# Gated mix of sliding-window attention and SwiGLU FFN: two tail tiles made behind the last exponential, output buffers swapped, WD rows and gate sums moved

## The chip, the core and the metric

One core of a Trainium2 chip runs the kernel. Its engines work side by side, each through its own list of instructions in order: TensorE (PE; PEld is its weight load), VectorE (DVE), ScalarE (ACT), GpSimd (POOL) and SyncE (SP), which here only issues DMAs. The metric is the device time of one launch in microseconds. The median of 3 runs before is 842.95 us (842.54 to 843.75).

## What is computed

```python
# x: 2048 x 512; 32 heads of 16; window 256; FFN width 1792
g = sigmoid((x * gate_w).sum(-1, keepdims=True))
q, k, v = heads(x @ wqkv)
p = softmax(where(0 <= i - j < 256, q @ k.T / 4, -1e9))
a = concat(p @ v) @ wo
b = (silu(x @ w_gate) * (x @ w_up)) @ w_down
out = g * a + (1 - g) * b
```

All is in float32. Every large product is made of three products of a high and a low part (hi·hi, hi·lo, lo·hi), so each operand is first "split": a cast to its high part on ACT (L65) or DVE (L67), and a subtraction for the low part (L68) on DVE or POOL.

## The kernel before

The program is written out in the order in which each engine gets its work; no scheduler reorders it. The sequence 2048 is cut into 4 chunks of 512 columns (CH) or 16 blocks of 128 (NB), the heads into 8 groups of 4 (G), the FFN into 14 tiles of 128 (NF).

**Start** (up to L491). x, the value weights and the first query and key weights are loaded and split; `split_x(c)` splits a chunk's four pieces on ACT and DVE. `vproj(b)` makes the values of a block in a PSUM tile "pb" that ACT copies out (`put_v`, L395). `proj` makes queries and keys of a group; `stack` places them by twelve DMAs (L247, L248) into the slots QT and KT. `first`, the score products of group 0 (L263), is interleaved with the remaining value products.

**Slots** (loop at L595). Slot t = 0 to 127 does the first pass over the scores of group g+1 (L263, row maxima on DVE, L265) and the second pass of group g (L304, exponential on ACT L306, masks on POOL L308 and L311). In the last sixteen slots, t from g7 = 112, there is no first pass left. Four slots share one "unit": a projection of a later group or one side, gate or up, of an FFN tile (L215), 48 pairs of matmuls. A unit's four results are copied to buffers "ev" (ring of 5, `kept()`, L511) and, for the FFN, stored to DRAM (`raws`, L514). `prepare`, at quarter 3 of a unit's first slot, splits the next unit's weights (wh on ACT L65, wl on POOL L68) and fetches the following ones into "raw", a single buffer (L73, raw<-wgu).

At the first slot of each four, `av` multiplies weights and values of a finished chunk (L328) and `finish` post-processes it in five pieces spread over the four slots: ACT copies one PSUM half into "on" (L339), DVE adds the other half (L341), transposes into "ot" (L346), divides (L350, L351), transposes into "on" again (L355), and POOL stores that (od<-on, L356). The pool `osb` had one buffer of each name, so L339 of the next chunk writes the buffer that od<-on reads.

`later(t, hd, f)` places further work behind quarter hd of slot t. In the last slots this is: the gate sums (`gate_fetch` L541, `gate_block` L544, one a slot from slot 111), six rows of WD (`wd_early`: fetch into an "ev" buffer by L73, split on DVE one slot later, L67 and L68), and the first made tile of the tail (`first_tile`, L562: SiLU as exp, +1, reciprocal, two products on POOL, split).

**Tail** (from L633). For c in 4 chunks and n in 14 tiles: `hidden` computes silu(gate)·up from reloaded tiles (`load_kept`, got<-raws, L692) or, for the tile MADE = 2 of the order, from 24 matmuls in PSUM (L703); `halved` splits it (hh on ACT, hl on DVE); `step` multiplies it with WD into four PSUM accumulators (12 matmuls, L83 to L85). Rows of WD that were not loaded early are fetched during chunk 0 and split on DVE and POOL (`load_wd` with raw2), and so are the four pieces of WO on ACT and POOL. Tile 0 of chunk 0 came ready from the slots.

Of the kernel before, what the change touches and what calls it, by code (L numbers as in the profile page):

```python
# [9 lines left out]
F32 = mybir.dt.float32  # L10
F32R = mybir.dt.float32r
AF = mybir.ActivationFunctionType
ALU = mybir.AluOpType
# [20 lines left out]
def gated_mix(ctx, tc, xT, xn, w01, wqk, wv, wo, wgu, wd, gw, out):  # L34
# [54 lines left out]
    def run(gen, n=None):  # L89

        while n is None or n > 0:
            if next(gen, run) is run:
                break
            n = n and n - 1
# [74 lines left out]
    with ExitStack() as A:  # L169
# [163 lines left out]
        def finish(g, c):  # L333


            first, second = AV[g, c]
            both = osb.tile([P, CH], F32, name="on")
            lo = 0 if c else 64
            nc.scalar.copy(both[:, lo:], second[:, lo:])  # L339
            yield  # L340
            nc.vector.tensor_tensor(out=both[:, lo:], in0=first[:, lo:], in1=both[:, lo:], op=ALU.add)  # L341
            if lo:
                nc.vector.tensor_copy(both[:, :lo], first[:, :lo])
            yield
            ot = osb.tile([P, CH], F32, name="ot")
            nc.vector.transpose(ot, both)  # L346
            yield
            v = ot.rearrange("p (s e) -> p s e", e=32)
            rc = osb.tile([P, CH // 32], F32, name="rc")
            nc.vector.reciprocal(rc, v[:, :, DH])  # L350
            nc.vector.tensor_tensor(out=v[:, :, :DH], in0=v[:, :, :DH],  # L351
                                    in1=rc[:, :, None].to_broadcast([P, CH // 32, DH]), op=ALU.mult)
            yield
            on = osb.tile([P, CH], F32, name="on")
            nc.vector.transpose(on, ot)  # L355
            nc.gpsimd.dma_start(od[g, :, c * CH:(c + 1) * CH], on)  # L356
            yield
# [56 lines left out]

        def split_x(c):
            for k in range(NK):
                split(xhi[c][:, k], xlo[c][:, k], xraw[c][k], nc.scalar, nc.vector)
# [27 lines left out]
        prefetch()  # L445
        split_x(1)
        fill_v(vs[1])
        fill_rows(QT[0], 0.0, 1, nc.gpsimd)
        fill_rows(KT[0], -1.0, 1, nc.gpsimd)
        for b in range(2):  # L450
            run(vproj(b))
        split_x(2)
        run(vproj(2))
        run(proj(0, 1, pp, "pa", los=nc.vector))
        stack(0, 0)
# [20 lines left out]
        for n, turn in enumerate(turns):  # L476
            for m, _ in enumerate(turn, 3 * NK * n):
                run(first, 2 * (2 * NB * (m + 1) // total - 2 * NB * m // total))
            if n == 3:
                prepare()  # L480
            if n == 8:
                put_max(0, 0)
            if n == 9:
                get_max(0, 0)
# [7 lines left out]
        ptp = A.enter_context(tc.tile_pool(name="ptp", bufs=13))  # L492
        osb = A.enter_context(tc.tile_pool(name="osb", bufs=1))

# [54 lines left out]

        pieces = [h for t in (*QT[0], KT[0][0], *QT[1], KT[1][0], KT[0][1]) for h in halves_of(t)]  # L550
        GATE0 = g7 - 1
        later(GATE0 - 1, 1, gate_place)
        for b in range(NB):
            later(GATE0 + b - 1, 3, lambda b=b: gate_fetch(b))
            later(GATE0 + b, 3, lambda b=b: gate_block(b))
        for m in range(6):
            wd_early(g7 + 3 + 2 * m, ORDER[m], pieces[m])

        hh0, hl0, g0, u0 = (KT[0][1][:, i * CH:(i + 1) * CH] for i in range(4))
        g0, u0 = g0.bitcast(F32), u0.bitcast(F32)  # L560

        def first_tile():  # L562
            e = kept()
            nc.scalar.activation(e, g0, AF.Exp, scale=-1.0)
            yield
            nc.vector.tensor_scalar(e, e, 1.0, None, op0=ALU.add)
            yield
            nc.vector.reciprocal(e, e)
            yield
            nc.gpsimd.tensor_tensor(out=e, in0=g0, in1=e, op=ALU.mult)  # L570
            yield
            nc.gpsimd.tensor_tensor(out=e, in0=e, in1=u0, op=ALU.mult)
            yield
            split(hh0, hl0, e, nc.scalar, nc.vector)
            yield
        FT = first_tile()

        def first_load():
            nc.sync.dma_start(g0, raws[0, 0, 0])
            nc.sync.dma_start(u0, raws[0, 1, 0])  # L580
        later(g7, 2, first_load)
        for m in (4, 5, 6, 8, 9, 11):
            later(g7 + m // 4, m % 4, lambda: run(FT, 1))

        def gate_done():
# [3 lines left out]
            nc.vector.tensor_scalar(igate, gate, -1.0, 1.0, op0=ALU.mult, op1=ALU.add)  # L589
        later(GATE0 + NB, 3, gate_done)  # L590

# [3 lines left out]
        for t in range(G * NB + 1):  # L595
# [29 lines left out]
            if t >= 10 and t % 4 == 2 and t + 6 < G * NB:  # L625
                load_v((t + 6) // 4)
        prepare()
        run(FIN)
# [4 lines left out]
    with ExitStack() as B:  # L633
# [108 lines left out]

        seq = [(c, n) for c in range(NCH) for n in range(NF)][1:]
        loads = [(c, ORDER[n]) for c, n in seq if n != MADE]
        for _ in range(3):
            load_kept(*loads.pop(0))
        fresh, waiting, ready = [], [(0, 0, hh0, hl0)], []
        for c, n in seq:
            f = ORDER[n]
            todo, ready = ready, []  # L750
            if c == 0 and n + 5 < NF:
                ready.append(load_wd(ORDER[n + 5], pieces[n + 5], raw2(), (nc.vector, nc.gpsimd)))
# [56 lines left out]
```

## Time and profile before

| what | us |
|---|---|
| median of 3 runs | 842.95 |
| the profiled execution | 845.21 |
| its span, first to last instruction | 843.5 |
| start, up to the first slots | about 0 to 90 |
| slots 112 to 127 with their last products | 541.6 to 613.0 |
| tail | 613.0 to 843.5 |
| mean granted clock of TensorE | 0.991 |

How the views are read. A busy line gives time, share of the span and number of instructions. A row of waits reads "engine, tile, line <- what ended the wait: us in total, times, longest". A row of the timeline reads "start, duration, engine, line, operation, tiles, count [idle time before it <- what ended it]". A row of windows reads "stretch, its length, then busy time and count of PE, PEld, DVE, ACT and POOL, granted clock, DMA share, GB/s".

### The profile page before, as it was taken

To read this page: it belongs to the slowest core of one execution; us is meant where nothing else is said; L and a number is where in the kernel's file an instruction comes from. 1 tells how busy PE (TensorE), PEld (TensorE's weight loads), DVE (VectorE), ACT (ScalarE), POOL (GpSimd) and SP (SyncE) were. 2 spreads that over 40 slices of the span, in tenths; PEclk is the share of its full clock that TensorE was granted. 3 is DMA by queue.
4 is the path that set the end of the run, shared out by engine and by line. 5 is a ranking of instruction groups with operands and counts; after the bars stand their busy time and mean duration, and the time that the engine had idled before them with its cause. 6 is when DMAs were issued, how large, how long until landed. Compare 5 with 4: busy or idle time off the path is not lost.

```text
span 843.5 us, 21585 instructions
## 1 busy us (share of the span) xinstructions
PE 826.2 (98%) x8306; PEld 688.2 (82%) x8306; DVE 516.7 (61%) x1416; ACT 448.2 (53%) x935; POOL 362.0 (43%) x645
## 2 busy tenths in 40 slices
PE   8999999999999999999999999999988999999998
PEld 5799988888898888888888888867766888888886
DVE  5496677677577667667667676654558344353433
ACT  6313666666666666656666665645444533344341
POOL 5812546555555646546555554565435211011020
PEclk9999999999999999999999999989999999999999
DMA  8664524534624624533633642546478735473721
GB/s 286 172 199 132 165 104 150 173 112 130 198 91 138 192 106 124 179 137 109 187 131 94 196 149 100 181 140 217 156 277 267 209 131 161 165 212 86 242 72 50
DMA packets 70582, 133.27 MB, mean 158 GB/s; under 512 B 14288, under 2 KB 19024, under 8 KB 70480
## 3 DMA queue, kind: packets, MB, share of 16 engines
q1 hardware_dynamic: 66512, 118.00, 44.9%
q0 software_dynamic: 3968, 13.90, 4.5%
q8 instruction: 65, 1.06, 0.5%
q14 instruction: 37, 0.30, 0.1%
HBM read 61.08 MB, written 45.61 MB: 126 GB/s over the span
## 4 chain that ended last, share of the span: by engine, by line
PE 84%; DMA 5%; POOL 4%; issue 2%; DVE 2%; SPq 2%; ACT 1%; POOLq 0%; ACTq 0%
PE pb L215 22%; PE pa L215 21%; PE pb L328 6%; PE ps L263 6%; PE ps L85 5%; PE ps L83 5%; PE ps L84 5%; PE ps L304 4%; PE pb L85 2%; PE pb L84 2%; PE pb L83 2%; PE ps L328 2%; DMA ev<-wd 1%; PE pb L703 1%; PE pa L703 1%
## 5 line engine op out<-in xcount | busy, mean ns | idle before, releaser
L265 DVE CUSTOM_DVE_ANT_0 ps<-ps,mask 128x384 f32<-128x384 f32 (+2 forms) x512 | 271.8, 539 | 144.3 <-PE ps L263 71.5
L306 ACT ACTIVATE pt<-ps 128x384 f32<-128x384 f32 (+2 forms) x512 | 240.7, 477 | 114.9 <-PE ps L263 56.9
L308 POOL TENSOR_SCALAR_AFFINE_SELECT pt<-pt 128x256 f32<-128x256 f32 x256 | 107.5, 420 | 228.3 <-ACT pt L306 219.8
L304 PE MATMUL ps<-q,k 64*128 64x384 f32 (+2 forms) x512 | 164.4, 330 | 2.4 <-ACT on L339 1.6
L263 PE MATMUL ps<-k,q 63*128 63x384 f32 (+2 forms) x512 | 159.9, 330 | 1.2 <-DMA k<-xhi 1.2
L215 PE MATMUL pb<-xhi,wh 64*128 64x512 f32 x512 | 117.8, 397 | 0.6 <-DVE on L341 0.6
L215 PE MATMUL pb<-xlo,wh 64*128 64x512 f32 x512 | 116.1, 394 | 0.0
L215 PE MATMUL pb<-xhi,wl 64*128 64x512 f32 x512 | 115.7, 394 | 0.0
L215 PE MATMUL pa<-xhi,wh 64*128 64x512 f32 x512 | 114.2, 395 | 0.8 <-ACT ev L511 0.8
L215 PE MATMUL pa<-xlo,wh 64*128 64x512 f32 x512 | 112.7, 393 | 0.0
L215 PE MATMUL pa<-xhi,wl 64*128 64x512 f32 x512 | 112.5, 393 | 0.0
L263 PEld LDWEIGHTS ps<-k,q 63*128 63x128 f32 x512 | 90.1, 185 | 16.0 <-issue 6.9
L304 PEld LDWEIGHTS ps<-q,k 64*128 64x128 f32 x512 | 93.6, 185 | 10.0 <-ACT on L339 2.5
L311 POOL TENSOR_SCALAR_AFFINE_SELECT pt<-pt 128x256 f32<-128x256 f32 x224 | 96.4, 430 | 0.0
L707 DVE TENSOR_TENSOR sg<-got,sg 128x512 f32<-128x512 f32 x51 | 51.3, 1005 | 52.6 <-ACT sg L706 48.2
L328 PE MATMUL ps<-pt,vg 64*32 64x320 f32 (+4 forms) x1408 | 76.5, 351 | 0.0
L328 PE MATMUL pb<-pt,vg 64*32 64x320 f32 (+3 forms) x1360 | 75.6, 356 | 0.0
L265 DVE DVE_READ_ACCUMULATOR2_ANT mx<- 128x1 f32 x512 | 71.5, 140 | 0.0
L328 PEld LDWEIGHTS pb<-pt,vg 64*32 64x32 f32 x1360 | 46.9, 107 | 29.3 <-ACT pt L306 9.9
L215 PEld LDWEIGHTS pb<-xhi,wh 64*128 64x128 f32 x512 | 60.4, 187 | 9.8 <-DVE on L341 1.1
L215 PEld LDWEIGHTS pb<-xhi,wl 64*128 64x128 f32 x512 | 60.5, 186 | 7.4
L215 PEld LDWEIGHTS pa<-xhi,wh 64*128 64x128 f32 x512 | 58.0, 186 | 8.2 <-ACT ev L511 1.9
(163 smaller groups left out, 1592.0 us busy)
## 6 DMA issues: line engine op xcount, KB each, us to landing
raws<-ev SPq DMA_DIRECT2D x104, 256.0 KB
got<-raws SPq DMA_DIRECT2D x102, 256.0 KB
od<-on POOLq DMA_DIRECT2D x32, 256.0 KB, 2.9
raw<-wgu SPq DMA_DIRECT2D x28, 256.0 KB
q<-xhi SPq DMA_DIRECT2D x56, 128.0 KB
k<-xhi SPq DMA_DIRECT2D x56, 128.0 KB
vd<-vs POOLq DMA_DIRECT2D x8, 672.0 KB, 5.0
vg<-vd SPq DMA_DIRECT2D x32, 168.0 KB
```

Source lines behind the costliest of these rows:

```text
L83: nc.tensor.matmul(ps, lh, rh, start=start and i == 0, stop=False)
L84: nc.tensor.matmul(ps, lh, rl, start=False, stop=False)
L85: nc.tensor.matmul(ps, ll, rh, start=False, stop=stop and i == n - 1)
L215: mm = nc.tensor.matmul(ps[me], w[r], x[r], start=not second and i == 0, stop=bool(second) and i == n - 1)
L263: nc.tensor.matmul(ps[:, :n], QT[g % 2][pr][r, q0:q0 + P], KT[g % 2][pr][r, k0:k0 + n], start=True, stop=True)
L265: mx = nc.vector.tensor_tensor_reduce(out=ps[:, :n], in0=ps[:, :n], in1=mask[:, 3 * P - n:], scale=1.0, scalar=NEG, op0=ALU.add, op1=ALU.m ...
L304: nc.tensor.matmul(ps[:, :n], KT[g % 2][pr][r, k0:k0 + P], QT[g % 2][pr][r, k0:k0 + n], start=True, stop=True)
L306: BEHIND.append(nc.scalar.activation(pt[:, j, :n], ps[:, :n], AF.Exp, scale=SCALE))
L308: nc.gpsimd.affine_select(out=pt[:, :, :P], in_=pt[:, :, :P], pattern=[[0, 2], [1, P]], compare_op=ALU.is_ge, fill=0.0, base=0, channel_mu ...
L311: nc.gpsimd.affine_select(out=pt[:, :, 2 * P:], in_=pt[:, :, 2 * P:], pattern=[[0, 2], [-1, P]], compare_op=ALU.is_ge, fill=0.0, base=-1, ...
L328: nc.tensor.matmul(AV[g, c][h][32 * j:32 * j + 32, q0 - c * CH:q1 - c * CH], VG[4 * g + kb // 4][o, kb % 4, 17 * j:17 * j + 32], PT[g, kb, ...
L707: nc.vector.tensor_tensor(out=sg, in0=gu[1], in1=sg, op=ALU.mult)
```

## The change

**Start.** `split_x` takes a range of pieces; chunks 1 and 2 are split two pieces at a time between `vproj(0)`, `vproj(1)` and `vproj(2)`, and `first` begins eight yields of the value products later. ACT, between its copies of the value results (vs_115 and vs_116 are the two value buffers, xhi_74 and xhi_76 the high parts of chunks 1 and 2), as a piece of the difference:

```order
 L65 CAST wh<-vs_116 128x512 x2
-L65 CAST xhi_74<-q_123 128x512 x4
-L395 COPY vs_115<-pb 128x8x4x16 x2
-L65 CAST xhi_76<-k_124 128x512 x4
+L65 CAST xhi_74<-q_123 128x512 x2
+L395 COPY vs_115<-pb 128x8x4x16
+L65 CAST xhi_74<-q_123 128x512 x2
+L395 COPY vs_115<-pb 128x8x4x16
+L65 CAST xhi_76<-k_124 128x512 x2
 L395 COPY vs_116<-pb 128x8x4x16
+L65 CAST xhi_76<-k_124 128x512 x2
 L238 COPY ev<-pa 128x512
```

The first copy has moved ahead of two casts; the third now has two casts behind it, ahead of L238, the copy that feeds `stack`.

**Slots.** In `finish`, all three tiles have the name "on" in a pool of two buffers; "rc" keeps one. Each chunk takes three buffers in turn, so the second half copy of a chunk and its stored result share a buffer, the tile between them has the other, and the next chunk begins with that other one. Nine WD rows instead of six are fetched, at slots 113 to 115, 117 to 119 and 121 to 123, and the order of the places they go to (`pieces`) is changed. The gate sums begin at slot 110. DVE in slots 117 to 121, before (q_87 is a place for WD rows, L544 a gate sum):

```order
L351 TENSOR_TENSOR ot<-ot,rc 128x16x16
L67 CAST q_86<-ev 128x512
L68 TENSOR_TENSOR q_86<-ev,q_86 128x512
L544 SCALAR_TENSOR_TENSOR xhi,gate<-xlo,xhi 128x512
L355 STREAM_TRANSPOSE on<-ot 128x512
L544 SCALAR_TENSOR_TENSOR xhi,gate<-xlo,xhi 128x512
L67 CAST q_87<-ev 128x512
L68 TENSOR_TENSOR q_87<-ev,q_87 128x512
L341 TENSOR_TENSOR on<-pb,on 128x512
L544 SCALAR_TENSOR_TENSOR xhi,gate<-xlo,xhi 128x512
```

and in the same place after (L546 is the gate sum):

```order
L351 TENSOR_TENSOR on<-on,rc 128x16x16
L67 CAST q_87<-ev 128x512
L68 TENSOR_TENSOR q_87<-ev,q_87 128x512
L546 SCALAR_TENSOR_TENSOR xhi,gate<-xlo,xhi 128x512
L355 STREAM_TRANSPOSE on<-on 128x512
L67 CAST k_88<-ev 128x512
L68 TENSOR_TENSOR k_88<-ev,k_88 128x512
L546 SCALAR_TENSOR_TENSOR xhi,gate<-xlo,xhi 128x512
L67 CAST k_88<-ev 128x512
L68 TENSOR_TENSOR k_88<-ev,k_88 128x512
L341 TENSOR_TENSOR on<-pb,on 128x512
L546 SCALAR_TENSOR_TENSOR xhi,gate<-xlo,xhi 128x512
```

One split still stands ahead of L355; behind it there are now two, and the second of them is directly ahead of L341 of the next chunk.

**End of the slots.** `first_tile` is gone. Tiles 0 and 1 of chunk 0 are loaded at slot 126 into the gate's places (XG), their SiLU stands behind the last exponential, at quarter 0 of slot 128, after `prepare` for the last FFN tile (which stood behind the loop), and their product and split at quarter 2. ACT there before, from the last exponential on:

```order
L306 ACTIVATE pt<-ps_10580 128x128
L511 COPY ev<-pa 128x512
L586 ACTIVATE gate<-gate 128x16
L511 COPY ev<-pb 128x512
L339 COPY on<-ps_10607 128x512
L511 COPY ev<-pb 128x512
L65 CAST wh<-raw 128x512
L706 ACT_TABLE_LOAD
L706 ACTIVATE sg<-got_10695 128x512
L65 CAST hh<-sg 128x512
```

and after, behind the last exponential:

```order
L513 COPY ev<-pa 128x512
L585 ACTIVATE gate<-gate 128x16
L65 CAST wh<-raw 128x512
L574 ACT_TABLE_LOAD
L574 ACTIVATE ev<-xhi 128x512
L574 ACTIVATE ev<-xlo 128x512
L513 COPY ev<-pb 128x512
L339 COPY on<-ps_10621 128x512
L65 CAST k_89<-ev 128x512 x2
L513 COPY ev<-pb 128x512
L704 ACTIVATE sg<-pa 128x512
L704 ACTIVATE sg<-got_10711 128x512
```

The table load and two SiLUs (ev<-xhi, ev<-xlo) come ahead of the copies of the last unit's second half (L513, formerly L511) and of L339; the two casts (k_89) come ahead of the last of these copies. The tail starts with tile 2, the 24 products, and steps 0 and 1 follow them on PE; tile 1 is no longer reloaded there, and WD rows 6, 7 and 8 are no longer split there.

The diff, without its renumbering:

```diff
-            ot = osb.tile([P, CH], F32, name="ot")
+            ot = osb.tile([P, CH], F32, name="on")
...
-            rc = osb.tile([P, CH // 32], F32, name="rc")
+            rc = osb.tile([P, CH // 32], F32, name="rc", bufs=1)
...
-        split_x(1)
+        split_x(1, range(2))
         fill_v(vs[1])
         fill_rows(QT[0], 0.0, 1, nc.gpsimd)
         fill_rows(KT[0], -1.0, 1, nc.gpsimd)
-        for b in range(2):
-            run(vproj(b))
-        split_x(2)
+        run(vproj(0))
+        split_x(1, range(2, NK))
+        run(vproj(1))
+        split_x(2, range(2))
         run(vproj(2))
+        split_x(2, range(2, NK))
...
-                run(first, 2 * (2 * NB * (m + 1) // total - 2 * NB * m // total))
+                run(first, 2 * (2 * NB * max(m + 1 - 8, 0) // (total - 8) - 2 * NB * max(m - 8, 0) // (total - 8)))
...
-        osb = A.enter_context(tc.tile_pool(name="osb", bufs=1))
+        osb = A.enter_context(tc.tile_pool(name="osb", bufs=2))
...
-        pieces = [h for t in (*QT[0], KT[0][0], *QT[1], KT[1][0], KT[0][1]) for h in halves_of(t)]
-        GATE0 = g7 - 1
+        pieces = [h for t in (*QT[0], KT[0][0]) for h in halves_of(t)]
+        pieces += [halves_of(t)[hf] for hf in range(2) for t in (*QT[1], KT[1][0])] + halves_of(KT[0][1])
+        GATE0 = g7 - 2
...
-        for m in range(6):
-            wd_early(g7 + 3 + 2 * m, ORDER[m], pieces[m])
+        for m, t in enumerate((1, 2, 3, 5, 6, 7, 9, 10, 11)):
+            wd_early(g7 + t, ORDER[m], pieces[m])
...
-        for m in (4, 5, 6, 8, 9, 11):
-            later(g7 + m // 4, m % 4, lambda: run(FT, 1))
...
+        first_halves = [[KT[0][1][:, (2 * n + i) * CH:(2 * n + i + 1) * CH] for i in range(2)] for n in range(2)]
+        first_sg = []
         def first_load():
+            for n in range(2):
+                for i in range(2):
+                    nc.sync.dma_start(XG[2 * n + i], raws[n, i, 0])
+        def first_silu():
+            for n in range(2):
+                sg = kept()
+                first_sg.append(sg)
+                nc.scalar.activation(sg, XG[2 * n], AF.Silu)
+        def first_tiles():
+            for n, sg in enumerate(first_sg):
+                nc.vector.tensor_tensor(out=sg, in0=XG[2 * n + 1], in1=sg, op=ALU.mult)
+                split(*first_halves[n], sg, nc.scalar, nc.vector)
+        later(g7 + NB - 2, 2, first_load)
+        later(g7 + NB, 0, prepare, first_silu)
+        later(g7 + NB, 2, first_tiles)
...
-        later(GATE0 + NB, 3, gate_done)
+        later(g7 + NB - 1, 3, gate_done)
...
-        prepare()
         run(FIN)
...
-        seq = [(c, n) for c in range(NCH) for n in range(NF)][1:]
+        seq = [(c, n) for c in range(NCH) for n in range(NF)][2:]
...
-        fresh, waiting, ready = [], [(0, 0, hh0, hl0)], []
+        fresh, waiting, ready = [], [(0, n, *first_halves[n]) for n in range(2)], []
...
-            if c == 0 and n + 5 < NF:
+            if c == 0 and 9 <= n + 5 < NF:
```

More of the change, by code (lines that the diff above doesn't have):

```diff
@@ L413, in gated_mix, with split_x @@
         xraw = [[xraw[2 * c + k // 2][k % 2] for k in range(NK)] for c in range(NCH)]
-        def split_x(c):
-            for k in range(NK):
+        def split_x(c, ks=range(NK)):
+            for k in ks:
                 split(xhi[c][:, k], xlo[c][:, k], xraw[c][k], nc.scalar, nc.vector)
@@ L555, in gated_mix @@
             later(GATE0 + b, 3, lambda b=b: gate_block(b))
-        for m in range(6):
-            wd_early(g7 + 3 + 2 * m, ORDER[m], pieces[m])
[L559 to L576, printed above, removed]
-        def first_load():
-            nc.sync.dma_start(g0, raws[0, 0, 0])
-            nc.sync.dma_start(u0, raws[0, 1, 0])
-        later(g7, 2, first_load)
-        for m in (4, 5, 6, 8, 9, 11):
-            later(g7 + m // 4, m % 4, lambda: run(FT, 1))
+        for m, t in enumerate((1, 2, 3, 5, 6, 7, 9, 10, 11)):
+            wd_early(g7 + t, ORDER[m], pieces[m])
+        first_halves = [[KT[0][1][:, (2 * n + i) * CH:(2 * n + i + 1) * CH] for i in range(2)] for n in range(2)]
+        first_sg = []
+        def first_load():
+            for n in range(2):
[13 more added lines that the diff above has]
+        later(g7 + NB, 2, first_tiles)
         def gate_done():
```

## The prediction

> **What bounds the kernel now.** I read the page's busy times first, then who TensorE waits for, then windows around those waits.
>
> ```profile
> span 843.5 us, 21585 instructions
> PE 826.2 (98%) x8306; PEld 688.2 (82%) x8306; DVE 516.7 (61%) x1416; ACT 448.2 (53%) x935; POOL 362.0 (43%) x645
> ```
>
> TensorE (PE) is busy nearly throughout, so an edit pays only where PE stands still or runs slow. PE's own waits:
>
> ```profile
> PE ps L85 <- DVE hl L68: 2.7, 3, 1.5
> PE ps L83 <- ACT hh L65: 2.5, 2, 1.4
> PE ps L304 <- ACT on L339: 1.6, 2, 1.0
> ...
> PE ps L263 <- DMA k<-xhi: 1.2, 1, 1.2
> PE pb L195 <- ACT vs L395: 0.9, 1, 0.9
> PE ps L304 <- ACT pt L306: 0.8, 1, 0.8
> PE pa L215 <- ACT ev L511: 0.8, 1, 0.8
> PE pb L215 <- DVE on L341: 0.6, 2, 0.3
> ```
>
> They fall in three places: the start (L263, L195: 2.1 us), the last sixteen slots, 112 to 127 (L304, L215: 3.8 us), and the first steps of the FFN tail (L83, L85: 5.2 us). The window view shows that the last slots lose more than these gaps. Each row is four slots, from one end of the attention product L328 to the next: stretch, its length, busy time by engine, granted clock, DMA.
>
> ```profile
> 541.62:562.46 20.84, 19.24 (x181) 13.97 (x176) 12.02 (x18) 10.64 (x24) 12.98 (x20) 0.84 0.54 181
> 562.46:578.07 15.61, 15.61 (x212) 12.42 (x208) 8.21 (x18) 9.75 (x22) 9.08 (x18) 1.00 0.54 168
> 578.07:595.50 17.43, 16.52 (x214) 12.97 (x209) 8.24 (x17) 9.81 (x22) 9.82 (x19) 1.00 0.59 198
> 595.50:613.03 17.53, 16.18 (x200) 13.00 (x195) 7.16 (x16) 7.86 (x21) 7.25 (x12) 0.90 0.42 148
> ```
>
> The second row is a clean one: no idle PE, full clock, 15.61 us for the same matmuls. So four slots should take 15.6, and the others took 20.8, 17.4 and 17.5. The granted clock below 1 is the second loss:
>
> ```profile
> 552.14:555.55 3.41, 2.30 (x12) 1.02 (x8) 3.28 (x7) 2.68 (x7) 3.41 (x5) 1.00 0.48 163
> 555.55:562.38 6.83, 6.34 (x75) 3.65 (x75) 1.18 (x2) 1.70 (x4) 2.54 (x6) 0.50 0.65 232
> 599.93:603.34 3.41, 3.41 (x18) 2.85 (x20) 2.46 (x5) 1.38 (x4) 3.11 (x5) 0.50 0.06 17
> 620.41:623.82 3.41, 2.01 (x8) 1.06 (x7) 1.64 (x3) 2.64 (x5) 0.00 (x0) 1.00 1.01 375
> 647.71:651.12 3.41, 3.30 (x8) 2.63 (x9) 2.83 (x5) 2.31 (x4) 1.28 (x1) 0.50 0.93 296
> ```
>
> Three stretches ran at half clock, 6.83, 3.41 and 3.41 us long. The first stands right behind a window in which PE was busy for 2.30 us of 3.41, and the other two behind the L304 and L83 waits. At half clock a bound PE loses half: 3.4, 1.7 and 1.7 us.
>
> **The change part by part.** *The made tile leaves the slots.* Slots 113 and 114 lose an exponential, a DVE reciprocal, two GpSimd (POOL) products and a split.
>
> ```profile
> 546.40 3.31 DVE L568 RECIPROCAL ev<-ev 128x512 f32<-128x512 f32 x1
> 552.87 0.62 ACT L65 CAST k<-ev 128x512 fp32r<-128x512 f32 x1 [3.36 <-POOL ev L572]
> ```
>
> ScalarE (ACT) works in order: it stood 3.36 us at this cast with the exponentials queued behind it, PE ran dry, and the clock halved. Nothing takes that place in these slots, so the first four fall from 20.84 to 15.61: −5.2.
>
> *Output buffers.* Here is the loop that costs the third and fourth rows 1.8 and 2.2 us:
>
> ```profile
> 562.66 0.53 ACT L339 COPY on<-ps 128x448 f32<-128x448 f32 x1 [5.42 <-PE ps L328]
> 565.18 1.76 POOL L68 TENSOR_TENSOR wl<-raw,wh 128x512 fp32r<-128x512 f32 x1
> 567.88 0.38 SPq L73 DMA_DIRECT2D ev<-wd  x1
> 569.83 2.09 SPq L73 DMA_DIRECT2D ev<-wd  x1
> 573.12 0.43 DVE L67 CAST q<-ev 128x512 fp32r<-128x512 f32 x1 [5.89 <-DMA ev<-wd]
> 574.80 0.70 DVE L355 STREAM_TRANSPOSE on<-ot 128x512 f32<-128x512 f32 x1
> 575.80 0.56 POOL L356 DMA_DIRECT2D od<-on  x1 [3.05 <-DVE on L355]
> 580.00 0.58 ACT L339 COPY on<-ps 128x512 f32<-128x512 f32 x1 [4.49 <-DMA od<-on]
> 581.84 0.71 DVE L346 STREAM_TRANSPOSE ot<-on 128x512 f32<-128x512 f32 x1
> ```
>
> The weight raw buffer is free only when POOL ends its split (566.94); the WD row queued behind it on SP goes out at 567.88 and lands at 573.12, 5.2 us later; VectorE (DVE) waits there with L355 behind it; L355's result is stored by od from the buffer that the next L339 overwrites, so L339 starts at 580.00 although its product ended at 578.07. After, L339 takes the other buffer: it needs L355's reading of it (575.50) and a store from one round earlier. By these rows the copy is free 2.6 us before it is due, and the clean 15.6 should hold. What is late next is L346, which now waits for od (landed by 580.0; L346 began at 581.84): hidden. If the gain fails, L339 stays 1.9 us late.
>
> *Nine WD rows for six, gate sums a slot earlier.* Three rows per four slots instead of one or two: three more fetches on SP, and three more pairs L67, L68 on DVE. A pair and a gate sum take 1.7 us together (573.12 to 574.80), so a pair is about 1.0; DVE is 8.2 us busy of 15.6. The third split now stands on DVE ahead of L341, which empties the PSUM that PE wants next. Counted from 562.66: L355 ends at 12.8, the second split and a gate sum at 14.5, the third split at 15.5; L341 can start at 16.0, after its copy (15.4 + 0.6). That is no delay if the third row has landed by 15.0. The second fetch of before was held on SP until 571.92 (9.3); with the same 5.2 us of flight the third lands at 14.5 or somewhat later. Per four slots the bounds are 0 and 5.2 (one more flight); I take the value near the first, 0.4, three times: +1.2. The gate sums keep their number; they add nothing while DVE has that room.
>
> Sum for the slots: 71.4 us before; after 3 × 15.6 + 15.3 (the last four have narrower exponentials) + 1.2 = 63.3: **−8.1**, with bounds −9.3 and −5.2.
>
> *The tail's start.* Before, steps 0 and 1 are split by 24 products, and then everything waits for the reloads:
>
> ```profile
> 610.54 0.45 PE L328 MATMUL pa<-pt,vg 64*32 64x320 f32 x1
> 614.24 0.32 SPq L514 DMA_DIRECT2D raws<-ev  x1
> 616.52 0.80 SPq L692 DMA_DIRECT2D got<-raws  x2
> 619.54 1.28 ACT L706 ACT_TABLE_LOAD   x1 [4.81 <-DMA got<-raws]
> 628.00 1.77 DVE L707 TENSOR_TENSOR sg<-got,sg 128x512 f32<-128x512 f32 x1
> 648.89 0.68 DVE L707 TENSOR_TENSOR sg<-got,sg 128x512 f32<-128x512 f32 x1
> 700.00:800.00 100.00, 100.00 (x443) 82.80 (x442) 42.35 (x59) 36.52 (x64) 8.24 (x7) 1.00 0.54 170
> ```
>
> A full matmul takes 100/443 = 0.226 us. From the end of the last attention product (call it T0, before 613.03) PE will now do the 24 products (5.4 us) and steps 0 and 1 (12 matmuls, 2.7 us, each), all ready early, so step 2 is due at T0 + 10.8. Its half tile is behind the first reload. ACT's copies and casts of a tile take 0.6 (580.00, 552.87). In its order: wh until T0 − 1.9 (its buffer is free when slot 127's products end, T0 − 2.5: 610.54 to 613.03), table 1.28, two SiLUs, L513 and L339 until T0 + 1.8, two casts with DVE's low half and product between them until T0 + 4.4, the last L513 until T0 + 5.0. Its store goes at 5.0, reloads 2.3 us later (614.24 to 616.52), landing 3.0 later (616.52 to 619.54): T0 + 10.3; SiLU and the cast of step 2 until 11.5, the low half until about 12.3. So one stall of about 1.0 (0.7 for the cast, 0.3 to 0.4 more for the low half) replaces the L83 and L85 waits, 2.5 + 2.7 = 5.2, and the half clock of 1.7. The other stalls came from three WD splits that are gone: while they ran, L707 took 1.77 instead of 0.68. Five splits and four WO rows remain; I leave 0.5. **−5.4**, with bounds −6.9 (no stall) and −2 (waits of the old size stay and only the half clock and a little go).
>
> The Trainium skill (ScalarE: Activation LUTs, "What ACT_TABLE_LOAD costs") says a switch costs about 2.66 us, 1.28 for the load and 1.38 for a drain ahead of it. The load agrees with 1.28; ACT was idle before it, so this trace can't show the drain. By that page the stall would be 2.4, and the total 1.4 worse.
>
> *The start.* ACT's first copy at L395 comes two casts (1.1 us) sooner, and the first score products eight yields later.
>
> ```profile
> 24.38 0.59 ACT L395 COPY vs<-pb 128x512 f32<-128x512 f32 x1 [2.89 <-POOL vs L381]
> 36.97 2.64 DMA k<-xhi
> ```
>
> That removes the 0.9. But this copy, the third, still waits for POOL until 24.38, and two casts now follow it, so the stack's first DMA goes up to 1.1 later and k<-xhi (landing 39.6) with it. The eight yields, 1.8 us of PE work, go ahead of that wait. Gain between 0.7 and 2.1; **−1.2**.
>
> Sum: −8.1 − 5.4 − 1.2 = −14.7. The profiled execution took 845.2 us (span 843.5 and 1.7 around), so 830.5 for one like it; the median of the runs shown, 842.95, is 2.3 below, so **828.3**.
>
> **Rivals.** *The copy stays late*: WD rows land later under more DMA, L355 passes 15.6, and rows three and four keep 1.8 and 2.2: 832.3. For: three fetches in a row; against: 2.6 us to spare. *The half clock stays*: the 13.7 us at 0.50 come of low activity that the edits don't touch, and 6.8 us return: 835.1. For: the window 620.41 to 623.82 has PE busy for only 2.01 us, and no half clock follows, so gaps alone don't decide. Against: all three stretches begin behind waits of the lists above. The Trainium skill (TensorE: Matmul & The Clock Gate, "HAM oscillation — how this bites in real kernels") speaks for this rival: it puts the limit at gaps over about 3.4 us, and none here reached half of that. *The reloads come 3 us later still* than my count: 831.3. *Slower*: the three fetches are served one behind the other, 5.2 us each, so the third lands at 10.5 + 10.4 = 21 and L341, behind its split, at 22 instead of 16: +6 three times, 846. It decides against the change from a third landing at about 20.5. Against it: raw<-wgu, raws, WD and xn left SP within 2 us and WD still took 5.2. *The change not doing what it says*: L339 waiting for the same store would read as the first rival.
>
> **How the numbers follow.** Forecast 0.57, late copy 0.15, half clock 0.12, late reloads 0.08, slower 0.05, no net change 0.03. What two runs of this kernel can tell apart is about 0.2%, 1.7 us. Faster 0.92, same 0.03, slower 0.05. The forecast's own bounds with their 0.4 to 1.2 us of choices reach 823; with the half clock 835.5: those two are the range.
>
> **What would show it.** Right: L339 waiting for PE alone, four slots at 15.6 to 16, no 0.50 stretch between slots 112 and 127, one PE gap of about 1 us at step 2, L707 at 0.7 in the first steps. Wrong: L339 behind od, L341 behind a WD split by microseconds, a table load with a drain, k<-xhi landing after 41.

## Result, and the profile after

| | before | after |
|---|---|---|
| median | 843.35 (842.54 to 846.14, 4 runs) | 832.44 (830.9 to 834.81, 4 runs) |
| profiled execution | 845.21 | 831.44 |
| its span | 843.5 | 829.7 |

The ratio is 0.9867, with a 95% interval from 0.9832 to 0.9902. The interval lies wholly below 1, so the kernel is faster, by 1.3%; the median is inside the predicted range of 823.0 to 835.5, 4.1 us above the predicted 828.3.

From the page after, the span and the busy times, and behind them the waits of TensorE (PE):

```profile
span 829.7 us, 21564 instructions
PE 816.6 (98%) x8306; PEld 677.6 (82%) x8306; DVE 512.3 (62%) x1418; ACT 448.1 (54%) x935; POOL 355.2 (43%) x640
```

```profile
PE pb L215 <- DVE on L343: 1.8, 1, 1.8
PE ps L263 <- DVE mx L265: 1.7, 1, 1.7
PE pa L175 <- POOL ident masks.py:199: 1.4, 1, 1.4
PE ps L83 <- ACT hh L65: 1.3, 1, 1.3
PE ps L263 <- DMA k<-xhi: 1.2, 1, 1.2
PE ps L85 <- DVE hl L68: 1.0, 2, 0.7
```

Both L304 rows and L195's wait for L395 are gone, the tail's rows fell from 5.2 to 2.3 us, and two rows are new: L263 behind DVE, and L215 behind L343. PE is 9.6 us less busy with as many matmuls; 6.8 of that, half of them, are put down to the 13.7 us at half clock, which are gone.

The window view by stretches of four slots, cut like the rows of before (end of one L328 product to the next); the first row is the four slots ahead of 112, the last the tail's first 36 us:

```profile
524.03:542.29 18.26, 16.50 (x225) 13.65 (x224) 11.82 (x38) 9.17 (x22) 6.46 (x14) 1.00 0.55 168
542.29:557.41 15.12, 15.12 (x179) 12.09 (x178) 7.38 (x15) 9.80 (x22) 8.26 (x16) 1.00 0.50 146
557.41:574.81 17.40, 15.65 (x210) 12.11 (x210) 12.39 (x25) 9.75 (x22) 11.55 (x21) 1.00 0.84 281
574.81:590.38 15.57, 15.57 (x210) 12.64 (x210) 9.66 (x19) 9.80 (x22) 10.57 (x18) 1.00 0.66 199
590.38:604.02 13.64, 13.64 (x196) 11.06 (x195) 5.06 (x13) 9.93 (x24) 7.92 (x13) 1.00 0.62 213
604.02:640.00 35.98, 33.50 (x142) 26.12 (x142) 26.29 (x35) 17.34 (x31) 12.39 (x9) 1.00 0.77 266
```

Three of the four slot rows have no idle PE and full clock. Together they take 61.7 us where before they took 71.4: −9.7. The tail takes 829.7 − 604.0 = 225.7 for 230.5: −4.8. Slot 112 begins 0.7 later (542.29 for 541.62), although the first attention product ends 1.2 sooner (98.6 for 99.8): the new wait at L263 lies between. Sum −13.8, which is 829.7 − 843.5.

Two rows hold the new waits: 1.8 us idle in 524 to 542, and 1.75 in 557 to 575. The first, as the timeline of DVE and that of SP show it (L546 is the gate sum, L540 and L543 its fetches):

```profile
534.89 0.69 DVE L546 SCALAR_TENSOR_TENSOR xhi<-xlo,xhi 128x512 f32<-128x512 f32 x1 [2.12 <-DMA vg<-vd]
```

```profile
528.10 0.33 SPq L73 DMA_DIRECT2D raw<-wgu  x1
528.49 0.42 SPq L516 DMA_DIRECT2D raws<-ev  x1
528.96 0.42 SPq L540 DMA_DIRECT2D xhi<-gw  x1
529.43 1.04 SPq L543 DMA_DIRECT2D xlo<-xn  x2
```

The first gate sum stands in slot 110, where the row maxima L265 of the last first pass stand behind it on DVE. DVE stood 2.12 us there and PE 1.7. The releaser named is a fetch of vg, which came last by the profile; what the gate sum reads are gw and xn, which left SP only after raw<-wgu at 528.10. That this queue is the cause is tested below.

The second, on DVE:

```profile
553.15 0.43 DVE L67 CAST q<-ev 128x512 fp32r<-128x512 f32 x1 [6.24 <-DMA ev<-wd]
...
556.25 0.43 DVE L67 CAST q<-ev 128x512 fp32r<-128x512 f32 x1 [0.72 <-DMA ev<-wd]
...
557.41 0.89 DVE L546 SCALAR_TENSOR_TENSOR xhi<-xlo,xhi 128x512 f32<-128x512 f32 x1
...
558.23 0.61 DVE L67 CAST q<-ev 128x512 fp32r<-128x512 f32 x1
558.88 1.49 DVE L68 TENSOR_TENSOR q<-ev,q 128x512 fp32r<-128x512 f32 x1
560.29 0.61 DVE L341 TENSOR_TENSOR on<-pb,on 128x448 f32<-128x448 f32 x1
```

ACT had copied its half by 558.02 (L339, below), but L341 began at 560.29: the third WD split stood ahead of it, itself late because the first two rows had landed late.

And what the change was to mend, in ACT's timeline:

```profile
557.48 0.54 ACT L339 COPY on<-ps 128x448 f32<-128x448 f32 x1 [2.16 <-PE ps L328]
...
574.84 0.59 ACT L339 COPY on<-ps 128x512 f32<-128x512 f32 x1 [2.68 <-PE ps L328]
...
590.42 0.59 ACT L339 COPY on<-ps 128x512 f32<-128x512 f32 x1 [2.67 <-PE ps L328]
```

L339 now waits for its product alone. The store od<-on ends a wait of DVE's L346 instead (0.65 us at 562.70), beside other work.

### The profile page after: what moved, and what is told of

Same layout as the page of the kernel before. It is cut to its first block, busy times and chain, and to the rows that moved or that the text cites. A ratio compares the mean times of both kernels' runs of the same rounds, so it can differ in the third digit from the quotient of the medians.

```text
span 829.7 us, 21564 instructions
## 1 busy us (share of the span) xinstructions
PE 816.6 (98%) x8306; PEld 677.6 (82%) x8306; DVE 512.3 (62%) x1418; ACT 448.1 (54%) x935; POOL 355.2 (43%) x640
## 4 chain that ended last, share of the span: by engine, by line
PE 86%; DMA 4%; POOL 3%; SPq 2%; DVE 1%; issue 1%; ACT 1%; POOLq 0%; ACTq 0%; DVEq 0%
PE pb L215 22%; PE pa L215 22%; PE pb L328 7%; PE ps L263 6%; PE ps L85 5%; PE ps L83 5%; PE ps L84 5%; PE ps L304 4%; PE pb L85 2%; PE pb L83 2%; PE pb L84 2%; PE ps L328 2%; PE pb L701 1%; PE pa L701 1%; DMA ev<-wv 1%
## 5 line engine op out<-in xcount | busy, mean ns | idle before, releaser
L265 DVE CUSTOM_DVE_ANT_0 ps<-ps,mask 128x384 f32<-128x384 f32 (+2 forms) x512 | 272.0, 539 | 144.1 <-PE ps L263 73.6
L263 PE MATMUL ps<-k,q 63*128 63x384 f32 (+2 forms) x512 | 159.4, 330 | 2.9 <-DVE mx L265 1.7
L304 PE MATMUL ps<-q,k 64*128 64x384 f32 (+2 forms) x512 | 161.3, 328 | 0.0
L215 PE MATMUL pb<-xhi,wh 64*128 64x512 f32 x512 | 112.8, 394 | 1.8 <-DVE on L343 1.8
L215 PE MATMUL pb<-xlo,wh 64*128 64x512 f32 x512 | 111.6, 391 | 0.0
L215 PE MATMUL pb<-xhi,wl 64*128 64x512 f32 x512 | 111.5, 392 | 0.0
L215 PE MATMUL pa<-xhi,wh 64*128 64x512 f32 x512 | 110.6, 394 | 0.0
L215 PE MATMUL pa<-xlo,wh 64*128 64x512 f32 x512 | 109.4, 391 | 0.0
L215 PE MATMUL pa<-xhi,wl 64*128 64x512 f32 x512 | 109.2, 391 | 0.0
L263 PEld LDWEIGHTS ps<-k,q 63*128 63x128 f32 x512 | 89.5, 185 | 21.0 <-issue 7.0
L304 PEld LDWEIGHTS ps<-q,k 64*128 64x128 f32 x512 | 91.9, 185 | 4.6 <-issue 0.8
L705 DVE TENSOR_TENSOR sg<-got,sg 128x512 f32<-128x512 f32 x50 | 48.4, 969 | 51.6 <-ACT sg L704 48.2
L328 PE MATMUL ps<-pt,vg 64*32 64x320 f32 (+4 forms) x1408 | 75.2, 346 | 0.0
L328 PE MATMUL pb<-pt,vg 64*32 64x320 f32 (+3 forms) x1360 | 74.0, 350 | 0.1
L265 DVE DVE_READ_ACCUMULATOR2_ANT mx<- 128x1 f32 x512 | 72.0, 141 | 0.0
L328 PEld LDWEIGHTS pb<-pt,vg 64*32 64x32 f32 x1360 | 46.4, 106 | 28.2 <-ACT pt L306 9.9
L215 PEld LDWEIGHTS pb<-xhi,wh 64*128 64x128 f32 x512 | 57.2, 185 | 11.0 <-DVE on L343 2.1
L215 PEld LDWEIGHTS pb<-xhi,wl 64*128 64x128 f32 x512 | 57.2, 184 | 7.7
L215 PEld LDWEIGHTS pa<-xhi,wl 64*128 64x128 f32 x512 | 55.4, 184 | 8.2
```

Of the source, the lines that this page charges most:

```text
L215: mm = nc.tensor.matmul(ps[me], w[r], x[r], start=not second and i == 0, stop=bool(second) and i == n - 1)
L263: nc.tensor.matmul(ps[:, :n], QT[g % 2][pr][r, q0:q0 + P], KT[g % 2][pr][r, k0:k0 + n], start=True, stop=True)
L265: mx = nc.vector.tensor_tensor_reduce(out=ps[:, :n], in0=ps[:, :n], in1=mask[:, 3 * P - n:], scale=1.0, scalar=NEG, op0=ALU.add, op1=ALU.m ...
L304: nc.tensor.matmul(ps[:, :n], KT[g % 2][pr][r, k0:k0 + P], QT[g % 2][pr][r, k0:k0 + n], start=True, stop=True)
L328: nc.tensor.matmul(AV[g, c][h][32 * j:32 * j + 32, q0 - c * CH:q1 - c * CH], VG[4 * g + kb // 4][o, kb % 4, 17 * j:17 * j + 32], PT[g, kb, ...
L705: nc.vector.tensor_tensor(out=sg, in0=gu[1], in1=sg, op=ALU.mult)
```

## The experiments

Ten kernels: seven are the changed kernel with one part altered, one is the kernel before with one part alone, and two put edits together. Times are compared with runs of the kernel before on the same chip; where a microsecond decides, the profile is read.

### The output buffers, undone

```diff
-            ot = osb.tile([P, CH], F32, name="on")
+            ot = osb.tile([P, CH], F32, name="ot")
...
-        osb = A.enter_context(tc.tile_pool(name="osb", bufs=2))
+        osb = A.enter_context(tc.tile_pool(name="osb", bufs=1))
```

> Against the changed kernel's profile (span 829.7 us), with the old roles of the output buffers (one buffer each of on, ot, rc) and all else as changed. Theory: the loop through od<-on comes back: L339 is again ended by DMA od<-on and stands 1.8 to 2.2 us late in the second, third and fourth four slots, 17.4 us each instead of 15.6 and 13.6; together +3.5 to +6 us, and a half clock stretch may come behind one of the waits. Rival (the made tile's removal alone made the room): L339 waits for PE as now, the four slots stay at 15.1, 17.4, 15.6 and 13.6, within 0.5 us.

Measured: 842.65 median (840.23 to 847.03, 10 runs), ratio to the kernel before 1.0004 [0.9977, 1.0031]. The whole gain is gone. The windows of the profiled execution (span 838.3), and ACT:

```profile
560.67:582.84 22.17, 19.32 (x211) 15.23 (x210) 11.84 (x24) 9.75 (x22) 11.92 (x20) 0.85 0.64 215
```

```profile
564.74 0.53 ACT L339 COPY on<-ps 128x448 f32<-128x448 f32 x1 [6.46 <-DMA od<-on]
```

The loop through od is back, but not as expected. It costs mainly in one row, not in three: 22.2 us, where the changed kernel took 17.4 and a row without waits 15.6. The copy is 4.1 us behind its product (560.67), PE waits 2.7 at L304, and 6.8 us at half clock follow. The expectation, 3.5 to 6, was too small: +8.6 by the profile. Of that 4.8 lie in this row and 0.7 in the last four slots (14.4 for 13.6); 1.7 are a half clock behind the gate sum, which the changed kernel's profile doesn't have, and 1.3 arose ahead of slot 108, 0.7 of them in the start.

### The output buffers alone, on the kernel before

The same lines the other way round in the kernel before, nothing else.

> The kernel before with only the output buffers' new roles. Theory (the loop through od<-on costs its rows by itself): the four slots go from 20.8, 15.6, 17.4, 17.5 to 20.8, 15.6, 15.6, 15.6 and the half clock behind the last L339 wait goes: -3.7 to -4, near 839. Rival (L339 was late because of the made tile's delay too, and the loop only shows beside it): third row 15.6 but first and fourth unchanged, -2 or less.

Measured: 837.73 (835.77 to 840.76, 10 runs), 0.9953 [0.9933, 0.9973], or −4.6. The windows:

```profile
541.21:560.63 19.42, 17.79 (x178) 12.78 (x178) 12.20 (x18) 10.64 (x24) 13.00 (x20) 0.91 0.56 188
560.63:576.24 15.61, 15.61 (x211) 12.73 (x210) 8.30 (x18) 9.75 (x22) 9.96 (x18) 1.00 0.57 185
576.24:591.84 15.60, 15.60 (x211) 12.78 (x210) 8.78 (x17) 9.81 (x22) 9.63 (x18) 1.00 0.66 215
591.84:605.47 13.63, 13.63 (x196) 10.82 (x195) 6.76 (x16) 7.97 (x21) 6.64 (x12) 1.00 0.47 166
```

As the theory has it, the waits of the last two rows go: 17.4 and 17.5 become 15.6 and 13.6, and the tail stays at 836.3 − 605.5 = 230.8. The first row is shorter too, 19.4 for 20.8, because one step of 3.41 us at half clock follows the cast's delay instead of two; that this comes of the swap isn't shown. So the swap by itself is worth 4.6 us between the medians, and in the changed kernel 10 (842.65 for 832.44). That it is worth more there because nine WD rows load DVE and the DMA queues is likely, but no run tests it.

### The old made tile, put back

```diff
+        def old_tile():
+            e = kept()
+            nc.scalar.activation(e, g0, AF.Exp, scale=-1.0)
...
+            split(hh0, hl0, e, nc.scalar, nc.vector)
...
+        for m in (4, 5, 6, 8, 9, 11):
+            later(g7 + m // 4, m % 4, lambda: run(FT, 1))
```

> The changed kernel with the work of the old made tile put back in slots 113 and 114 beside the new tiles (two loads, exponential, +1, reciprocal, two GpSimd products, split); its result is overwritten later. Theory: ACT stands at the cast L65 behind POOL's products with exponentials queued, PE waits at L304 and the first four slots go from 15.1 to 18.3 without and 20.8 with a half clock behind it. Rival (what cost there was the old buffer loop, not the tile): the first four slots stay at 15.1 to 16.

Measured: 836.3 (833.72 to 840.08, 10 runs), 0.9917 [0.989, 0.9943]. The windows, and ACT:

```profile
543.29:564.05 20.76, 19.15 (x179) 13.65 (x178) 14.73 (x22) 10.64 (x24) 13.73 (x20) 0.84 0.55 178
```

```profile
554.47 0.62 ACT L65 CAST k<-ev 128x512 fp32r<-128x512 f32 x1 [3.36 <-POOL ev L594]
```

The first four slots take 20.8 again, with the same 3.36 us of ACT behind POOL and the same 6.83 us at half clock (556.98 to 563.80). That term of the prediction holds, and without the old buffers. What it is worth varies with the clock: the five runs at 0.999 or 1.000 took 833.7 to 834.9 us, 1 to 2.5 more than the changed kernel's median, and the five at 0.991 to 0.994 took 837.7 to 840.1, or 5 to 8 more.

### Seven WD rows ahead instead of nine

```diff
-        for m, t in enumerate((1, 2, 3, 5, 6, 7, 9, 10, 11)):
+        for m, t in enumerate((1, 2, 5, 6, 9, 10, 11)):
...
-            if c == 0 and 9 <= n + 5 < NF:
+            if c == 0 and 7 <= n + 5 < NF:
```

> The changed kernel with seven WD rows fetched early (slots 113, 114, 117, 118, 121, 122, 123) instead of nine; rows 7 and 8 are split in the tail again, in its first steps. Theory (the rows' splits on DVE stretch L705 to 1.78 us and so make the tail's waits): the second four slots fall from 17.4 to 15.6, the tail grows from 225.7 by 0.5 to 2, with new L83 and L85 gaps between 607 and 620; the whole stays within 1.5 us of the changed kernel. Rival (the rows were most of the tail's gain): the tail goes back towards 230, +3 or more.

Measured: 835.4 (834.23 to 838.69, 9 runs), 0.993 [0.9908, 0.9953]. The second four slots did fall to 15.65, but the tail took 833.9 − 603.1 = 230.8: the rival. DVE in the tail:

```profile
618.03 0.43 DVE L67 CAST q<-raw 128x512 fp32r<-128x512 f32 x1 [4.01 <-DMA raw<-wd]
```

and two windows behind each other there, in the first of which PE is busy for 0.05 us:

```profile
614.63:618.05 3.42, 0.05 (x1) 0.00 (x0) 0.01 (x1) 1.14 (x2) 0.00 (x0) 1.00 0.93 275
618.05:624.88 6.83, 5.76 (x14) 4.51 (x15) 6.83 (x9) 3.03 (x5) 4.25 (x3) 0.50 0.97 352
```

Nothing was slow about the split. DVE stood 4.0 us for a row whose fetch had left SP at 612.66, behind six reloads; PE stood 4.4 us at L85 and ran 6.83 us at half clock behind that. The 1.78 us of L705, on which the theory rested, were not what cost. The tail is as long as that of the kernel before (230.5), although tiles 0 and 1 are made early here too. So the two early tiles do not win the tail's time without the rows; no run leaves them out, and what they are worth by themselves stays open.

### Gate fetches ahead of raw<-wgu

```diff
-        later(GATE0 - 1, 1, gate_place)
+        later(GATE0 - 2, 1, gate_place, lambda: gate_fetch(0))
```

> gw and the first block of xn are fetched at quarter 1 of slot 108, ahead of the fetch raw<-wgu, which waits on SP for its buffer; all else as changed. Theory: the 1.7 us gap at 536 us (L263 waiting for DVE, where the first gate sum waits for its DMA) was that queue: it goes, span -1.7 (828.0). Rival (the gate sum itself, or DMA load, is late): the gap stays between 1.2 and 1.7, or moves to the next gate sum.

Measured: 830.53 (830.0 to 832.78, 4 runs), 0.9868 [0.9833, 0.9904], which doesn't tell it from the changed kernel. In the profile (828.6) the gap at L263 is gone and slots 108 to 112 take 16.28 us for 18.26. SP fetched xn at 520.14, and the gate sum began without a wait:

```profile
532.62 0.69 DVE L546 SCALAR_TENSOR_TENSOR xhi<-xlo,xhi 128x512 f32<-128x512 f32 x1
```

So the fetches' place behind raw<-wgu in SP's queue was the cause of that wait.

### Third WD split behind L341

```diff
-            later(t, 2, lambda: later(t + 1, 2, load_wd(f, piece, kept())))
+            later(t, 2, lambda: later(t + 1, 2 + (t % 4 == 3), load_wd(f, piece, kept())))
```

> The third WD split of each four slots stands one quarter later, behind L341 of the next chunk. Theory: the 1.75 us gap at 561 us (L215 waiting for L343) goes and the second four slots take 15.6 instead of 17.4; the other rows stay, since there L341 already follows its copy: span -1.8 (827.9). Rival (L341 is late because the first two splits waited for WD behind q<-mxd on SP): the gap shrinks by less than half.

Measured: 830.59 (829.88 to 834.88, 5 runs), 0.9862 [0.9823, 0.9902]. The profiled execution (span 833.2) was the slowest of the five. Its window for the second four slots:

```profile
558.74:574.41 15.67, 15.67 (x210) 12.52 (x210) 9.94 (x23) 9.76 (x22) 12.12 (x21) 1.00 0.85 281
```

The gap is gone, as the theory says. But the gap also varies by itself: in the profiles with the third split ahead of L341 and two buffers it is 1.75 (the changed kernel), 1.76 (old start), 0.89 (gate fetches ahead) and 0.15 (WO later), and with the old made tile put back there is none. In all three profiles with the split behind L341, this one and the two of the edits together, there is none either. That the order is the cause fits all of them, but the size isn't explained. The span is no gain here, because this execution had two stretches at half clock, behind the gate sum and in the tail.

### WO fetched together and split two steps later

```diff
-            if c == 0 and n >= 6 and n % 2 == 0:
-                ready.append(load_wo((n - 6) // 2))
+            if c == 0 and 9 <= n < 13:
+                wos[divmod(n + 2, NF)] = [load_wo(n - 9)]
```

The pieces under `wos[c, n]` are split in the step (c, n). What it is to mend, in ACT's timeline of the changed kernel:

```profile
613.24 0.63 ACT L704 ACTIVATE sg<-got 128x512 f32<-128x512 f32 x1 [2.18 <-DMA got<-raws]
...
625.25 0.62 ACT L65 CAST woh<-raw 128x512 fp32r<-128x512 f32 x1 [3.71 <-DMA raw<-wo]
625.77 0.61 ACT L65 CAST hh<-sg 128x512 fp32r<-128x512 f32 x1
...
632.97 0.62 ACT L65 CAST woh<-raw 128x512 fp32r<-128x512 f32 x1 [4.84 <-DMA raw<-wo]
633.49 0.61 ACT L65 CAST hh<-sg 128x512 fp32r<-128x512 f32 x1
```

> The four pieces of WO are fetched in steps 9 to 12 of the tail's first chunk and split two steps behind their fetch, instead of fetched at 6, 8, 10, 12 and split one step behind. Theory: ACT no longer waits 3.7 and 4.8 us for raw<-wo with the casts hh behind it, the four PE gaps between 626 and 636 (2.5 us) go: span -2.0 to -2.5. Rival (the gaps come of DVE, where L705 takes 1.78 us beside five WD splits): the gaps at 626 to 628 stay and only those at 634 and 635, at most 2.0, go; or ACT waits for WO again two steps later and nothing is won.

Measured: 827.7 (827.03 to 828.25, 4 runs), 0.9829 [0.9796, 0.9862]. The window over the tail's start, and ACT:

```profile
602.45:640.00 37.55, 37.31 (x161) 29.92 (x162) 30.18 (x38) 18.80 (x33) 13.50 (x9) 1.00 0.82 275
```

```profile
641.13 0.62 ACT L65 CAST woh<-raw 128x512 fp32r<-128x512 f32 x1 [2.56 <-DMA raw<-wo]
```

PE idles 0.24 us here, for 2.5 us of the changed kernel's 36. The tail takes 825.3 − 602.5 = 222.8, or 2.9 less. ACT still waits for WO, 0.83 us at 636.90 and 2.56 at 641.13, but no gap of PE follows. L705 took as long as before and PE didn't wait for it: the rival falls.

### The start, undone

The diff is the start's part of the change, reversed.

> The changed kernel with the start of before (split_x whole, first not moved). Theory: PE's wait at L195 for the copy L395 (0.9) is back, the gap before k<-xhi stays at 1.2, and the first attention product ends 1.2 us later (99.8 for 98.6): +1.2. Rival (the eight yields were the gain, not the copy): L195 waits, but the k<-xhi gap grows too, +2.

Measured: 834.69 (833.36 to 835.93, 4 runs), 0.9913 [0.989, 0.9935]. In the profile (831.6) the L195 wait for L395 doesn't show, and the k<-xhi gap is 1.2, as in the changed kernel. The first attention product ends at 99.4; in the profiles with the new start it ends between 98.1 and 99.6 (eight of them, mean 98.8), with the old one between 99.3 and 99.8 (three, mean 99.5). The start is worth about 0.7 by that. The median is 2.2 above the changed kernel's, but it was taken on another chip, and the intervals of the two ratios overlap. Theory and rival are not told apart, and as L195 doesn't wait for L395 here although the start is the old one, the new order isn't shown to be what removed that wait.

### All three edits together, and a fourth in the start

> The three edits together on the changed kernel: first gate fetches ahead of raw<-wgu, third WD split behind L341, WO fetched in steps 9 to 12 and split two steps later. Theory (the three gaps are separate): slot 108 to 112 takes 16.3 us, the four slots 15.0, 15.6, 15.6, 13.6, the tail 222.9; no PE gap over 1 us behind the start, so no half clock either, and all runs lie close together: span 823 us, median 824.5 to 825.5, a range under 1.5 us. Rival (one gap comes back elsewhere, since the transfers only change places): 827 or more, with a half clock stretch in some runs.

Measured: 825.31 (824.86 to 826.33, 4 runs), 0.9803 [0.9785, 0.9822], which lies wholly below the interval of the changed kernel. Its windows, cut as above:

```profile
524.93:541.22 16.29, 16.24 (x225) 13.73 (x224) 11.74 (x38) 9.17 (x22) 7.00 (x14) 1.00 0.53 176
556.26:571.92 15.66, 15.66 (x211) 12.63 (x210) 10.66 (x23) 9.75 (x22) 11.92 (x21) 1.00 0.86 280
601.13:640.00 38.87, 37.99 (x165) 30.50 (x165) 30.40 (x38) 18.80 (x33) 13.53 (x9) 1.00 0.80 273
```

The waits of the first two rows are gone. In the tail one of 0.9 us at L85 is left, and the tail takes 824.6 − 601.1 = 223.5. The granted clock is 1.0 in all four runs, and they lie within 1.5 us.

The fourth edit puts the last two casts of chunk 2 behind `stack(0, 0)`:

```diff
         run(vproj(2))
-        split_x(2, range(2, NK))
         run(proj(0, 1, pp, "pa", los=nc.vector))
         stack(0, 0)
+        split_x(2, range(2, NK))
```

> As the three edits together, and in the start the last two casts of chunk 2 stand behind proj(0, 1) and stack(0, 0), no longer between the third copy L395 and the copy L238. Theory (these casts hold up the stack, as the prediction has it): the first stack DMA goes 1.1 us sooner and the gap before L263 at 40.5 us (1.2 to 1.4) shrinks to 0.1 to 0.4: about 1 us less than the three edits. Rival (SP's queue sets it: the issues from 29 to 35 us take 1.6 to 1.9 us each beside the stores vd<-vs): k<-xhi lands within 0.3 us of now and the gap stays.

Measured: 825.19 (824.7 to 826.87, 4 runs), 0.9804 [0.9784, 0.9824]. PE's wait for k<-xhi, in the timelines of the three edits and of the four:

```profile
41.44 0.33 PE L263 MATMUL ps<-k,q 63*128 63x128 f32 x2 [1.70 <-DMA k<-xhi]
```

```profile
39.98 0.33 PE L263 MATMUL ps<-k,q 63*128 63x128 f32 x2 [0.51 <-DMA k<-xhi]
```

The wait fell by 1.2, but kernels whose start is that of the change show it at anything from under 0.1 to 1.7, and the times don't differ: whether those two casts matter stays open. Either of these two kernels beats the changed one by 0.6%.

## Why the prediction was right, and where it was off

**Direction and places: right.** L339 waits for PE alone, no half clock stands between slots 112 and 127, and the gain lies where it was forecast: slots −9.7 (forecast −8.1), tail −4.8 (−5.4). In the profiled executions the change is −13.8 for a forecast of −14.7. That these two are so close is in part luck: the last four slots came out 1.7 us shorter than the 15.3 of the sum, and a wait of 1.7 us that the sum doesn't have came in at the gate sum. The slots' own bounds, −9.3 and −5.2, don't hold −9.7, and the second doesn't follow from "0 and 5.2" per four slots, which three times would reach +6.3.

**The made tile, −5.2: right for an execution with half clock behind it.** The four slots went from 20.84 to 15.12, and to 20.76 with the tile put back. In half of the runs with the tile put back the mean clock was 0.999 or 1.000, and the tile cost 1 to 2.5.

**The output buffers, 1.8 and 2.2: right in mechanism, and in size for the first** (17.4 to 15.6 when made alone). The second was 3.9 (17.5 to 13.6): the last four slots, 15.3 in the sum, take 13.64, so that term was mis-sized by 1.7. The row of before already showed it, for without its idle time of PE (1.35) and its half clock (1.7) its 17.53 are 14.5. They hold 196 matmuls where the row before them holds 210; at that row's mean this accounts for about 1.0, and the rest is left open.

**The third split, 0.4 three times: mis-sized.** It was 1.75 once and nothing twice in the changed kernel's profile, and from none to 1.76 in that one place in the other profiles with this order. The mark set for "wrong", L341 behind a WD split by microseconds, did appear in one place of three. The first fetch there left SP at 550.37, behind four fetches q<-mxd that only the first unit has, and the time line was counted from a unit without them.

**"The gate sums keep their number; they add nothing while DVE has that room": the step that failed.** It asked whether DVE had room, not what the first sum waits for and who stands behind it. Slot 110 still has a first pass, so PE's next scores stood behind a DMA: 1.7 us, and 3.4 where a half clock followed.

**The tail's start, −5.4: near, with two wrong terms that cancel in part.** The stall of 1.0 at step 2 isn't there: the SiLU of step 2 began at 613.24, T0 + 9.2, where the count had the reload at T0 + 10.3. In one other profile, with the gate fetches ahead, 0.35 us shows there. "I leave 0.5" for the other stalls was 2.3 to 2.5. It blamed WD splits and the slow L707; the runs showed fetches that land behind their split, WO on ACT here, WD on DVE with seven rows. And the forecast laid the gain mainly to the two early tiles; the run with seven rows has them too, and its tail is as long as before, though 3.4 us of that are half clock. The profile before had the WO waits already (3.56 and 4.56 us on ACT at 637.58 and 645.18), and I read past them.

**The start, −1.2: agrees, but by luck as far as the runs show.** The first attention product ends 1.2 us sooner in the profile of the changed kernel than in that of before (98.6 for 99.8). Profiles with the same new start differ by 1.5 us among themselves, and the mean difference of the two starts is 0.7. The 0.9 at L195 is 0.5 in one and nothing in the other of the two further profiles with the old start. In one of the eight profiles with the new start, that of the three edits, k<-xhi landed at 41.2 us, where a landing after 41 was named as a sign of being wrong. The chain of the changed kernel's profile reaches this fetch through POOL's fills and through issues on SP that take 1.7 to 1.8 us each (29.2 to 34.5), not through ACT's two casts, which the prediction had as the cost; what makes the issues so long wasn't tested.

**The table load.** By the Trainium skill (ScalarE: Activation LUTs, "What ACT_TABLE_LOAD costs") 1.38 us of drain stand beside the load's 1.28. The page doesn't say on which side; the prediction put them ahead of it. ACT in the changed kernel:

```profile
601.34 0.62 ACT L65 CAST wh<-raw 128x512 fp32r<-128x512 f32 x1 [0.18 <-PE pb L215]
601.98 1.28 ACT L574 ACT_TABLE_LOAD   x1
603.27 0.63 ACT L574 ACTIVATE ev<-xhi 128x512 f32<-128x512 f32 x1
```

The load begins 0.02 us behind a busy instruction and the SiLU 0.01 behind the load: 1.28 in all, and no drain on either side. That alternative falls.

**From the profile to the median: the largest error.** The sum was made against the profiled execution, 845.21, and then 2.3 us were taken off because the median lay that much lower. But that execution had 13.7 us at half clock, and the same sum had just removed them: what set it apart from the median was taken off twice. 44 runs of the kernel before, from three series, sorted by their mean granted clock:

| clock | runs | median us | from, to |
|---|---|---|---|
| 0.998 to 1.000 | 13 | 840.3 | 839.0, 841.7 |
| 0.995 to 0.997 | 16 | 842.9 | 839.5, 844.7 |
| 0.994 and less | 15 | 844.7 | 842.8, 846.9 |

The profiled execution had 0.991. Its group lies 1.8 us above the middle one, about as much as the 2.3 that were taken off; that the two are the same loss is inferred from this table. Without that step the forecast is 830.5. Of the 4.1 us of error 2.2 are this, 0.9 the sum, and 1.0 is the changed kernel's own profile, which at full clock lay below its median. The 44 runs spread from 839.0 to 846.9, so the 0.2% or 1.7 us that the prediction took for the noise of this kernel was too little; it had three runs to go by.

The rivals: the copy wasn't late, the reloads came sooner rather than later, and the three fetches were not served one behind the other: the rows of DVE above have the first at 553.15 and the third by 558.23, where 10.4 us between them were feared. *The half clock stays* was partly right: not in the profiled execution, but the four runs of the changed kernel spread over 3.9 us at clocks of 0.997 to 1.000, and the profiles of three other kernels with its gate wait show the clock halved behind it. Where the clock fell in the changed kernel's other runs isn't recorded.

## What to carry to other kernels

When an edit moves a wait, look for what the moved instruction itself waits for and for who is queued behind it on its engine, not whether its engine has room: gate sum, third split and WO cost mainly by late DMA, not by their own time. In this tail a split two steps behind its fetch took the idle time of the bound engine from 2.5 us to 0.24; one step (2.7 us) is shorter than the two late fetches of WO took (3.2 and 4.3 us from issue to split). Convert a profiled sum to a median only after asking what made the profiled run differ, and whether the sum removes just that.

## What was not expected of the hardware

The granted clock changes in steps of 3.41 us: every stretch at half clock that ends within one of the twelve profiles is 3.41 or 6.83 us long. Whether it halves doesn't depend on the length of a gap alone. The same gate wait in slot 110 in two kernels whose slots 108 to 112 are alike; the rows are two steps one behind the other (length, PE busy, PEld busy, ..., clock). With the output buffers undone, where PE stood 1.93 us until 537.69:

```profile
534.65:538.07 3.42, 1.49 (x15) 1.02 (x14) 1.67 (x7) 0.71 (x2) 0.41 (x1) 1.00 0.65 243
538.07:541.48 3.41, 3.41 (x21) 3.07 (x20) 2.62 (x10) 1.30 (x4) 0.95 (x2) 0.50 0.67 231
```

and with seven WD rows, where PE stood 1.97 us until 537.10:

```profile
532.71:536.13 3.42, 2.42 (x24) 1.83 (x20) 1.04 (x5) 1.42 (x4) 0.82 (x2) 1.00 0.81 283
536.13:539.54 3.41, 2.44 (x24) 2.27 (x26) 3.41 (x12) 1.32 (x4) 0.98 (x2) 1.00 0.37 126
```

The first gap lies in one step: PE was busy for 1.49 us of it, and the next step ran at half clock, 1.7 us more lost. The second, as long, is cut by a step's edge, leaves 2.4 us of work in each, and nothing followed. Over the profiles of this study, each of the ten steps at full clock whose weight loads (PEld) were busy for 1.04 us or less of 3.41 was followed by half clock, and none with 1.27 or more; of the six between, three were. PE's own busy time sorts them less well: a step with 2.47 us was followed by half clock and one with 1.75 wasn't. That is a pattern of these traces; no run was made to test it. The Trainium skill (TensorE: Matmul & The Clock Gate, "HAM oscillation — how this bites in real kernels") puts the limit at gaps over about 3.4 us; here single gaps of 1.8 to 1.9 us were followed by half clock in three profiles. So a gap of 1.8 us on a bound PE costs its own length or about twice that (1.7 us more), by where it falls, and with such gaps gone the runs of the three edits together lay within 1.5 us of each other.
